# Value products, row-sum product and shift rows in tiles of 32 output columns, and one mask product placed earlier

## The chip, the core and the metric

The kernel runs on one core of one Trainium2 chip. A core has a matrix engine (TensorE; PE in the profile, with its weight loads shown apart as PEld), a vector engine (VectorE, DVE), an activation engine (ScalarE, ACT), a general engine (GpSimd, POOL) and an engine that issues transfers (SyncE, SP). SBUF is the working memory, PSUM the memory into which TensorE writes its products. The metric is the device time of one execution in microseconds; less is better.

## The reference: what is computed

Two blocks follow one another. The first is attention with routing, for 4 batches of 8 heads, 768 positions, head size 64:

```
q_assign = argmax(q_n @ c_n.T);  k_assign = argmax(k_n @ c_n.T)     # 16 centroids a head
mask     = q_assign[:, None] == k_assign[None, :]
scores   = where(mask, q @ k.T / 8, -1e9)
attn     = exp(scores - rowmax);  attn = attn / (sum(attn) + 1e-9)
out      = attn @ v
```

Its output, seen as x of 3072 tokens by 512, goes into the second block, `g = h * erf(softplus(h))` with `h = x @ w_in` (512 by 2048), and `out = g @ w_out` (2048 by 512). All matrices are float32.

## The kernel before, in words

Heads are taken in pairs (`e` = 0, 1 on partitions 0 to 63 and 64 to 127): 16 pairs `p`. Within a pair the queries are two halves of `HW` = 384 columns and the keys six tiles `j` of 128, so that a pair has 12 units (pair, half, j). A unit's scores stand with keys on partitions and queries along the free axis, `[128, 2, 384]`. The main loop is `period(p, i)`, i = 0 to 5, which carries two units u and u+1. Each engine executes in the order in which the code emits (the wrapper `InOrder`), and no planner moves anything. In a period, in the order of emission on TensorE:

- `turn` (in i = 0 and 3): six small products of `lowest`, the row maxima of three query tiles, bring the shifts of a half into a row; two ACT copies put it into `qm`.
- `step_ahead(u)`: for the next half to come, a tile of 128 queries by 384 keys in bf16 into the one PSUM tile `wide`, two products `qv,kv` and two mask products `qm,km`; DVE takes the row maximum (`nmx`).
- `products(u)`, `products(u+1)`: the float32 scores, two matmuls a unit, into one of two PSUM tiles `sc`.
- `step_ahead(u+1, True)` in two parts, `scores(u)` beside its second, then `scores(u+1)`: bf16 mask products onto the scores.
- `mask(place)`: `MASKS` says in which period and at which of four places (0 to 3) the mask operands `qm`, `km` of the next pair are made, by one product of `hotT` and `pick` into a `turned` tile and one copy (on DVE in i = 0, else on ACT). Before, the keys' first is at (0, 2), that is after `scores(u+1)`; its copy comes after that of the row maxima on DVE.
- `similarities(p+2)` (i = 3): four matmuls of 32 output columns by 384 moving columns, in tiles of 32 columns already.
- `curve(u)`, `curve(u+1)`: ACT's exponential of `sc` into one of eight SBUF tiles `pr`, each with two extra columns of a tiny constant behind the 384.
- `accumulate(u-2)`, `accumulate(u-1)`: POOL sums the `pr` tiles of a half over j into `acc`.
- `attend(u-2)`, `attend(u-1)` (the change's "second products"): v times `pr`, for each head one float32 matmul of 64 output columns by 386 moving columns, summed over j in the PSUM tile `turned[half]`.
- `divide` (i = 0 and 3, once a half): the "sums' product", `minus` (all -1, 64 columns) times `acc`, into `turned[1 - half]`. It gives the negative row sum, the same on all 64 partitions of a head. Then ACT makes the reciprocal by logarithm and exponential (`inv`), DVE makes `den`, scales the product in place (`raw`) and writes `x`, and SP sends `x` to the transposed activations `x_dram`. Its later parts are emitted in the next period.

Two `turned` tiles serve for attend's sums, the sums' product, the similarities, the masks and the shift rows. Beside all this ACT, DVE and POOL round the weights of the second block and make forms of them (until pair 11 or so, and from pair 12 on).

After pair 15 the second block runs on float32 products of 128 by 128 by 256, seven products for eight (`block`). Its first block of products comes before the last `divide` (`finish_attention`).

In the trace each float32 matmul shows as two passes, each with a weight load; a bf16 matmul is one pass. All work recorded by the wrapper has line 60.

Of the kernel before, what the change touches and what calls it, by code (L numbers as in the profile page):

```python
# [9 lines left out]
F32 = mybir.dt.float32  # L10
# [4 lines left out]
ALU = mybir.AluOpType  # L15
ACT = mybir.ActivationFunctionType
# [3 lines left out]
P = 128  # L20
B, H, S, D = 4, 8, 768, 64
C = 16
NJ = S // P
Q = 32
NB = S // Q
HW = S // 2
HJ = NJ // 2
HP = H // 2
NPAIR = B * HP
# [14 lines left out]
EPS = 2.0**-70  # L44
NPT = NJ + 2
N_LATE = 10
LAST_X = 11
MASKS = {(0, 2): ("k", 0), (2, 0): ("q", 0), (2, 2): ("k", 1), (5, 2): ("q", 1)}
FIRST_MASKS = {(2, 0): ("k", 0), (2, 1): ("q", 0), (2, 2): ("k", 1), (5, 2): ("q", 1)}


# [17 lines left out]
def kernel(  # L69
# [10 lines left out]
    nc = tc.nc  # L80

    in_order = [True]
    te, ve, ae, ge = (
        InOrder(tc, e, in_order) for e in (nc.tensor, nc.vector, nc.scalar, nc.gpsimd)
    )
# [4 lines left out]
    const = pool("const", 1)  # L90
# [3 lines left out]
    turned = [ps.tile([P, 512], F32, name=f"turned{i}") for i in range(2)]  # L94
# [3 lines left out]
    more_in = const.tile([P, 3, HK, DFF // 2], F32, name="more_in")  # L98
    more_out = const.tile([P, 3, HF, HM], F32, name="more_out")
    x_more = const.tile([P, 3, HK, HT], F32, name="x_more")  # L100
    minus = const.tile([P, D], F32, name="minus")
    alleps = const.tile([P, 1], F32, name="alleps")
    x_dram = dram.tile([DM, B * S], F32, name="x_dram")

# [8 lines left out]
    const = passing("fixed", 1)  # L113
    stage = passing("stage", 1)
    vp = passing("vp", 2)
    routep = passing("routep", 1)
# [18 lines left out]
    def part_of(i, lo, n):  # L135
        return more_out[:, i].rearrange("p f m -> p (f m)")[:, lo : lo + n]
# [1 line left out]
    rows = [{nm: const.tile([P, S], F32, name=f"{nm}T{i}") for nm in "qk"} for i in range(2)]  # L138
    rows.append({"q": part_of(1, 2 * HW, S), "k": part_of(2, 2 * HW, S)})

    prs = [const.tile([P, 2, HW + 2], F32, name=f"pr{i}") for i in range(NPT)]


    pairs = {}
# [31 lines left out]
        load(p, "k", k, stage if p != 1 else None)  # L176


    setup = prs[-1].rearrange("p e n -> p (e n)")
    cen = setup[:, 0:D]  # L180
    sy.dma_start(out=cen, in_=centroids.rearrange("h c d -> (h c) d"))

# [6 lines left out]
    make_identity(nc, ident)  # L189
    ve.memset(ccT, 0.0)  # L190
    for t in prs:
        ge.memset(t[:, :, HW : HW + 2], EPS)

    ge.memset(first, -1.0)
    for base, pattern, sign, op, fill in (
# [67 lines left out]
    for e in range(2):  # L263
        for n in range(2):
            r = e * D + n * Q
# [9 lines left out]
        ge.memset(t, 0.0)  # L275

    cn = setup[:, D : 3 * D].rearrange("p (e d) -> p e d", e=2)
    spare = iter(range(3 * D, HW))

    def scalar_tile():  # L280
        n = next(spare)
# [73 lines left out]
    def masks(p, nm, half, bank, narrow=False, copied_by=ae):  # L355

        if p >= NPAIR:
            return lambda: None
        st = pairs[p]
        cols = slice(half * HW, (half + 1) * HW)  # L360
        r = slice(0, D) if nm == "q" else slice(D, P)
        if narrow:
            r = slice(r.start + half * Q, r.start + (half + 1) * Q)
        won = bank[:, 0:HW]
        te.matmul(won, lhsT=pick[r, half], rhs=st["hotT"][r], start=True, stop=True)
        if nm == "q":
            return lambda: ae.activation(out=st["qm"][:, cols], in_=won, func=ACT.Relu)
        if copied_by is ve:
            return lambda: ve.tensor_scalar(
                out=st["km"][:, cols], in0=won, scalar1=BIG, scalar2=nbig, op0=ALU.mult, op1=ALU.add  # L370
            )
        return lambda: ae.activation(
            out=st["km"][:, cols], in_=won, func=ACT.Identity, bias=nbig, scale=BIG
        )
# [3 lines left out]
    def maxima_step(p, i, sm=wide, behind=False):  # L378

        st = pairs[p]  # L380
        nmx = maxima[p % 2]
        t, half = divmod(i, 2)

        def passes(a, b, start, rows):
            for e in range(2):
                r = slice(e * D + rows.start, e * D + rows.stop)
                te.matmul(
                    sm[:, e, 0:HW], lhsT=st[a][r, t * P : (t + 1) * P],
                    rhs=st[b][r, half * HW : (half + 1) * HW], start=start, stop=not start,
                )  # L390

        passes("qv", "kv", True, slice(0, D))
        if behind:
            yield
        passes("qm", "km", False, slice(Q, D) if behind else slice(0, D))
        ve.tensor_reduce(
            out=nmx[:, :, t, half], in_=sm[:, :, 0:HW], axis=AX.X, op=ALU.max, negate=True
        )
        if i in (NJ - 1, 2 * NJ - 1):
            h = i // NJ  # L400
            ve.tensor_reduce(
                out=lowest[h][:, :, ::D].rearrange("p t e -> p e t"),
                in_=nmx[:, :, h * HJ : (h + 1) * HJ], axis=AX.X, op=ALU.min,
            )
            turns.append((p, h))

    def turn(p, h, copies=(ae.copy, ae.copy)):

        st = pairs[p]
        pn = turned[h][:, 0:HW].rearrange("p (t n) -> p t n", t=HJ)  # L410
        for t in range(HJ):
            for e in range(2):
                cols = slice(e * D, (e + 1) * D)
                te.matmul(pn[cols, t], lhsT=lowest[h][:, t, cols], rhs=identb, start=True, stop=True)
        for e, copy in zip(range(2), copies):
            r = slice(e * D, e * D + 1)
            copy(out=st["qm"][r, h * HW : (h + 1) * HW], in_=pn[r].rearrange("p t n -> p (t n)"))
        st["shift", h] = True
# [6 lines left out]
    sc_of = {}  # L425
# [14 lines left out]
    def scores(u):  # L440

        p, half, j = units[u]
        st = pairs[p]
        sc = sc_of[u]
        assert ("shift", half) in st
        for e in range(2):
            r = slice(e * D, (e + 1) * D)
            r = slice(r.start, r.start + Q)
            te.matmul(
                sc[:, e, 0:HW], lhsT=st["km"][r, j * P : (j + 1) * P],  # L450
                rhs=st["qm"][r, half * HW : (half + 1) * HW], start=False, stop=True,
            )

    def curve(u):

        pr = prs[u % NPT]
        ae.activation(out=pr[:, :, 0:HW], in_=sc_of.pop(u)[:, :, 0:HW], func=ACT.Exp, scale=D**-0.5)

    def accumulate(u):

        p, half, j = units[u]
        st = pairs[p]
        pr = prs[u % NPT]
        if j == 1:
            st["acc", half] = part_of(1 + half, 0, 2 * HW).rearrange("p (e t) -> p e t", e=2)
        if j > 0:
            acc = st["acc", half]
            so_far = prs[(u - 1) % NPT][:, :, 0:HW] if j == 1 else acc
            ge.tensor_tensor(out=acc, in0=so_far, in1=pr[:, :, 0:HW], op=ALU.add)

    def attend(u):

        p, half, j = units[u]
        st = pairs[p]
        if j == 0:
            st["av", half] = turned[half][:, 0 : HW + 2]
        for e in range(2):
            te.matmul(
                st["av", half][e * D : (e + 1) * D], lhsT=st["v"][:, j, e], rhs=prs[u % NPT][:, e],
                start=(j == 0), stop=(j == NJ - 1),  # L480
            )

    def divide(u):

        p, half, _ = units[u]
        st = pairs[p]
        av = st["av", half]

        psum = turned[1 - half][:, 0:HW]
        for e in range(2):  # L490
            te.matmul(
                psum[e * D : (e + 1) * D], lhsT=minus, rhs=st["acc", half][:, e], start=True, stop=True
            )

        if u + 1 < len(units):
            inv = routep.tile([P, HW], F32, name="inv")
            den = routep.tile([P, HW], F32, name="den")
        else:
            inv, den = part_of(0, 4 * HW, HW), part_of(1, 0, HW)
        ae.activation(out=inv, in_=psum, func=ACT.Ln, bias=alleps, scale=-1.0)  # L500
        ae.activation(out=inv, in_=inv, func=ACT.Exp, scale=-1.0)
        yield
        ve.scalar_tensor_tensor(
            out=den, in0=psum, scalar=S * EPS, in1=inv, op0=ALU.subtract, op1=ALU.mult
        )
        raw = av[:, 0:HW]
        ve.scalar_tensor_tensor(
            out=raw, in0=raw, scalar=av[:, HW : HW + 1], in1=inv, op0=ALU.add, op1=ALU.mult
        )
        yield  # L510
        x = part_of(0, (2 * p + half) % 4 * HW, HW)
        ve.scalar_tensor_tensor(out=x, in0=den, scalar=2.0, in1=raw, op0=ALU.add, op1=ALU.mult)
        b, r = divmod(p, HP)
        nc.sync.dma_start(
            out=x_dram[r * P : (r + 1) * P, b * S + half * HW : b * S + (half + 1) * HW], in_=x
        )
        if half == 1:
            del pairs[p]
        yield
# [222 lines left out]
    def period(p, i):  # L742
# [4 lines left out]
        def mask(place):  # L747
            which = (MASKS if p else FIRST_MASKS).get((i, place))
            if which:
                return masks(p + 1, *which, turned[0 if i in (0, 5) else 1], place > 1, ve if i == 0 else ae)  # L750
            return lambda: None

        if u > 0:
# [13 lines left out]
        second = step_ahead(u + 1, True) if u > 0 else iter(())  # L767
        next(second, None)
        scores(u)
        next(second, None)  # L770
        next(part[0], None)
        scores(u + 1)
# [59 lines left out]
                next(part[0])  # L832
        if i == 3 and early(n2):
            size(n2)
        mask(3)()


    def warm(n, bank, rhs):
# [176 lines left out]
```

## Time and profile before

| what | value |
|---|---|
| median of 3 runs | 1011.37 us (1010.65 to 1011.74) |
| the profiled execution | 1011.8 us |
| its span, first to last instruction | 1009.3 us |
| PE busy over the span | 1001.3 us (99%) |
| DVE, ACT, POOL busy over the span | 699.8, 501.6, 349.2 us |
| from 30 to 424 us (attention): PE, DVE, ACT, POOL busy | 394.0, 310.0, 288.5, 304.7 us of 394.0 |
| from 424 us to the end: PE busy | 581.8 us of 585.3 |
| granted TensorE clock | 1.00 |
| x_dram writes (line 514) | 32 of 192 KB, 2.0 us from issue to landing |

A group's row reads: engine and operation, out<-in by the program's names, the tile of the array in rows*columns and shapes, how many, busy time in us and the mean length of one in ns. Lengths of passes overlap: TensorE is pipelined, so the time that a pass costs is read from one start to the next and not from its length.

### The profile page before, as it was taken

To read this page: it belongs to the slowest core of one execution; us is meant where nothing else is said; L and a number is where in the kernel's file an instruction comes from. 1 tells how busy PE (TensorE), PEld (TensorE's weight loads), DVE (VectorE), ACT (ScalarE), POOL (GpSimd) and SP (SyncE) were. 2 spreads that over 40 slices of the span, in tenths; PEclk is the share of its full clock that TensorE was granted. 3 is DMA by queue.
4 is the path that set the end of the run, shared out by engine and by line. 5 is a ranking of instruction groups with operands and counts; after the bars stand their busy time and mean duration, and the time that the engine had idled before them with its cause. 6 is when DMAs were issued, how large, how long until landed. Compare 5 with 4: busy or idle time off the path is not lost.

```text
span 1009.3 us, 15518 instructions
## 1 busy us (share of the span) xinstructions
PE 1001.3 (99%) x5930; PEld 699.8 (69%) x5930; DVE 699.8 (69%) x1315; ACT 501.6 (50%) x659; POOL 349.2 (35%) x237
## 2 busy tenths in 40 slices
PE   8999999999999999999999999999999999999998
PEld 3444444444444444488888888888888888888887
DVE  8788888888788776869767564756565647565653
ACT  3777777777777665467623222232314050505050
POOL 1677777777777777853120000000000000000000
PEclk9999999999999999999999999999999999999999
DMA  9444444444344211042001100110001000000001
GB/s 208 90 104 103 104 102 101 104 104 106 84 106 101 55 33 32 23 169 84 0 1 43 43 1 1 42 42 1 21 22 42 0 22 21 1 1 21 22 1 42
DMA packets 141641, 55.55 MB, mean 55 GB/s; under 512 B 127104, under 2 KB 131456, under 8 KB 141568
## 3 DMA queue, kind: packets, MB, share of 16 engines
q1 hardware_dynamic: 139216, 54.28, 21.0%
q8 instruction: 46, 0.75, 0.3%
q10 hardware_dynamic: 2352, 0.30, 0.2%
q14 instruction: 27, 0.22, 0.1%
HBM read 41.98 MB, written 12.58 MB: 54 GB/s over the span
## 4 chain that ended last, share of the span: by engine, by line
PE 96%; DVE 2%; DMA 1%; SPq 0%; issue 0%; ACT 0%; DVEq 0%; ACTq 0%
PE bank L60 43%; PE turned L60 32%; PE sc L60 16%; PE wide L60 5%; DVE nmx L60 1%; DMA in_k<-in_k_dram 0%; SPq L60 0%; DMA in_q<-in_q_dram 0%; DVE x_own L60 0%; DVE more_in L60 0%; DVE x_more L60 0%; DVE w_in L60 0%; DVE kT L60 0%; DVE turned L60 0%; DVE sims L60 0%
## 5 line engine op out<-in xcount | busy, mean ns | idle before, releaser
L60 DVE TENSOR_REDUCE nmx<-wide 128x2 f32<-128x768 f32 x189 | 180.9, 957 | 80.7 <-PE wide L60 80.0
L60 POOL TENSOR_TENSOR more_out<-more_out,pr 128x768 f32<-128x768 f32 x128 | 216.4, 1691 | 28.7 <-ACT pr L60 22.8
L60 ACT ACTIVATE pr<-sc 128x768 f32<-128x768 f32 x192 | 148.8, 811 | 91.0 <-PE wide L60 86.6
L60 PE MATMUL turned<-pr,in_v 128*64 128x386 f32 x768 | 145.4, 500 | 0.0
L60 DVE TENSOR_TENSOR g<-bank,g 128x256 f32<-128x256 f32 x222 | 89.7, 422 | 53.1 <-PE bank L60 46.5
L60 PE MATMUL bank<-x_own,w_in 128*128 128x256 f32 x424 | 104.6, 380 | 0.5 <-DVE x_own L60 0.5
L60 PE MATMUL bank<-w_out,g 128*128 128x256 f32 x448 | 103.1, 379 | 0.0
L60 PE MATMUL sc<-qT,kT 64*128 64x384 f32 x528 | 98.2, 484 | 0.0
L60 PEld LDWEIGHTS turned<-pr,in_v 128*64 128x64 f32 x768 | 46.6, 136 | 69.9 <-issue 59.3
L60 PEld LDWEIGHTS bank<-w_out,g 128*128 128x128 f32 x448 | 85.1, 190 | 11.6
L60 PEld LDWEIGHTS bank<-x_own,w_in 128*128 128x128 f32 x424 | 80.3, 190 | 12.9 <-DVE x_own L60 0.9
L60 ACT COPY g<-bank 128x256 f32<-128x256 f32 x28 | 10.4, 372 | 152.4 <-PE bank L60 148.4
L60 DVE TENSOR_TENSOR osb<-bank,osb 128x256 f32<-128x256 f32 x87 | 35.5, 421 | 72.8 <-ACT osb L60 25.4
L60 ACT ACT_TABLE_LOAD x48 | 61.6, 1283 | 45.7 <-DVE g L60 45.1
L60 PE MATMUL bank<-x_more,more_in 128*128 128x256 f32 x296 | 76.0, 379 | 0.0
L60 PEld LDWEIGHTS <-qv 64*128 64x128 bf16 x384 | 26.8, 93 | 68.5 <-issue 52.5
L60 POOL TENSOR_TENSOR more_out<-pr,pr 128x768 f32<-128x768 f32 x32 | 59.3, 1854 | 28.4 <-ACT pr L60 28.4
L60 PEld LDWEIGHTS sc<-qT,kT 64*128 64x128 f32 x528 | 52.4, 187 | 19.9 <-ACT pr L60 1.2
L60 PE MATMUL wide<-kv,qv 64*128 64x384 bf16 x378 | 64.8, 328 | 1.1 <-ACT km L60 0.6
L60 PE MATMUL bank<-more_out,g_more 128*128 128x256 f32 x272 | 64.3, 379 | 0.0
L60 DVE TENSOR_TENSOR g<-a_s,g 128x512 f32<-128x512 f32 x96 | 62.5, 689 | 1.4 <-ACT a_s L60 1.4
L60 PE MATMUL wide<-km,qm 64*128 64x384 bf16 (+1 forms) x378 | 62.5, 327 | 0.0
(170 smaller groups left out, 1683.5 us busy)
## 6 DMA issues: line engine op xcount, KB each, us to landing
x_own<-in_moe_w_in_dram SPq DMA_DIRECT2D x13, 512.0 KB, 4.5
in_v<-in_v_dram SPq DMA_DIRECT2D x32, 192.0 KB, 2.9
x_dram<-more_out SPq DMA_DIRECT2D x32, 192.0 KB, 2.0
x_own<-x_dram SPq DMA_DIRECT2D x6, 1024.0 KB, 5.1
out_dram<-osb SPq DMA_DIRECT2D x23, 256.0 KB, 2.0
in_k<-in_k_dram SPq DMA_DIRECT2D x59, 96.0 KB, 2.7
in_q<-in_q_dram SPq DMA_DIRECT2D x58, 96.0 KB, 2.7
g_more<-in_moe_w_out_dram SPq DMA_DIRECT2D x6, 512.0 KB, 3.5
```

What stands on the lines that cost most here:

```text
L60: ins = getattr(self.engine, name)(*args, **kw)
```

## The change

It does five things. `pr` is laid out as quarters, for each head two runs of 192 queries with the two extra columns behind each (`TW` = 194). `attend` splits each head's matmul into four: two parts `k` of 32 output columns by two runs `c` of 194 moving columns; the four (head, run) combinations `g` go to the four 32-column tiles of the array, and `k` is placed along the free axis of PSUM. The sums' product uses `minus` with 32 columns and the four quarters of `acc` as moving operands, so it writes 32 equal rows for each quarter. What follows it works on that layout: `den` and `inv` have 192 columns, `raw` is two instructions, and `x` leaves in four transfers. `turn` takes 32 columns of `lowest` instead of 64. And the keys' first mask product moves from place 2 to place 3 of period 0, which now lies between `scores(u)` and `scores(u+1)`; its DVE copy comes before the row maximum of `step_ahead(u+1)`.

```diff
+QW = HW // 2
+TW = QW + 2
...
-MASKS = {(0, 2): ("k", 0), (2, 0): ("q", 0), (2, 2): ("k", 1), (5, 2): ("q", 1)}
+MASKS = {(0, 3): ("k", 0), (2, 0): ("q", 0), (2, 2): ("k", 1), (5, 2): ("q", 1)}
...
-    minus = const.tile([P, D], F32, name="minus")
+    minus = const.tile([P, Q], F32, name="minus")
...
-    prs = [const.tile([P, 2, HW + 2], F32, name=f"pr{i}") for i in range(NPT)]
+    prs = [const.tile([P, 2, 2, TW], F32, name=f"pr{i}") for i in range(NPT)]
...
         passes("qm", "km", False, slice(Q, D) if behind else slice(0, D))
+        if behind:
+            yield
         ve.tensor_reduce(
...
-                cols = slice(e * D, (e + 1) * D)
+                cols = slice(e * D, e * D + Q)
                 te.matmul(pn[cols, t], lhsT=lowest[h][:, t, cols], rhs=identb, start=True, stop=True)
...
-        ae.activation(out=pr[:, :, 0:HW], in_=sc_of.pop(u)[:, :, 0:HW], func=ACT.Exp, scale=D**-0.5)
+        sc = sc_of.pop(u)[:, :, 0:HW].rearrange("p e (c x) -> p e c x", c=2)
+        ae.activation(out=pr[:, :, :, 0:QW], in_=sc, func=ACT.Exp, scale=D**-0.5)
+
+    def quarters(t):
+        return t.rearrange("p e c n -> p (e c) n")[:, :, 0:QW]
...
-            st["av", half] = turned[half][:, 0 : HW + 2]
-        for e in range(2):
-            te.matmul(
-                st["av", half][e * D : (e + 1) * D], lhsT=st["v"][:, j, e], rhs=prs[u % NPT][:, e],
-                start=(j == 0), stop=(j == NJ - 1),
-            )
+            st["av", half] = turned[half][:, 0 : 2 * TW].rearrange("p (k n) -> p k n", k=2)
+        for k in range(2):
+            for g in range(4):
+                te.matmul(
+                    st["av", half][g * Q : (g + 1) * Q, k], lhsT=st["v"][:, j, g // 2, k * Q : (k + 1) * Q],
+                    rhs=prs[u % NPT][:, g // 2, g % 2], start=(j == 0 and k == 0), stop=(j == NJ - 1 and k == 1),
+                )
...
-        psum = turned[1 - half][:, 0:HW]
-        for e in range(2):
-            te.matmul(
-                psum[e * D : (e + 1) * D], lhsT=minus, rhs=st["acc", half][:, e], start=True, stop=True
-            )
+        psum = turned[1 - half][:, 0:QW]
+        for g in range(4):
+            te.matmul(psum[g * Q : (g + 1) * Q], lhsT=minus, rhs=st["acc", half][:, g], start=True, stop=True)
...
-        raw = av[:, 0:HW]
+        for k in range(2):
+            raw = av[:, k, 0:QW]
+            ve.scalar_tensor_tensor(
+                out=raw, in0=raw, scalar=av[:, k, QW : QW + 1], in1=inv, op0=ALU.add, op1=ALU.mult
+            )
+        yield
+        x = part_of(0, (2 * p + half) % 4 * HW, HW).rearrange("p (k x) -> p k x", k=2)
         ve.scalar_tensor_tensor(
-            out=raw, in0=raw, scalar=av[:, HW : HW + 1], in1=inv, op0=ALU.add, op1=ALU.mult
+            out=x, in0=den.unsqueeze(1).to_broadcast([P, 2, QW]), scalar=2.0, in1=av[:, :, 0:QW],
+            op0=ALU.add, op1=ALU.mult,
         )
...
-        nc.sync.dma_start(
-            out=x_dram[r * P : (r + 1) * P, b * S + half * HW : b * S + (half + 1) * HW], in_=x
-        )
+        for g in range(4):
+            rows_of, at = r * P + g // 2 * D, b * S + half * HW + g % 2 * QW
+            nc.sync.dma_start(
+                out=x_dram[rows_of : rows_of + D, at : at + QW].rearrange("(k r) x -> r k x", k=2),
+                in_=x[g * Q : (g + 1) * Q],
+            )
...
-                return masks(p + 1, *which, turned[0 if i in (0, 5) else 1], place > 1, ve if i == 0 else ae)
+                return masks(p + 1, *which, turned[0 if i in (0, 5) else 1], place > 1, ve if place == 3 else ae)
...
         scores(u)
+        next(second, None)
+        mask(3)()
         next(second, None)
         next(part[0], None)
         scores(u + 1)
...
         if i == 3 and early(n2):
             size(n2)
-        mask(3)()
```

More of the change, by code (lines that the diff above doesn't have):

```diff
@@ L176, in load_qk @@
         load(p, "k", k, stage if p != 1 else None)
-    setup = prs[-1].rearrange("p e n -> p (e n)")
+    setup = prs[-1].rearrange("p e c n -> p (e c n)")
     cen = setup[:, 0:D]
@@ L191 @@
     for t in prs:
-        ge.memset(t[:, :, HW : HW + 2], EPS)
+        ge.memset(t[:, :, :, QW:], EPS)
     ge.memset(first, -1.0)
@@ L277 @@
     cn = setup[:, D : 3 * D].rearrange("p (e d) -> p e d", e=2)
-    spare = iter(range(3 * D, HW))
+    spare = iter(range(TW, HW))
     def scalar_tile():
@@ L464, in accumulate @@
         if j == 1:
-            st["acc", half] = part_of(1 + half, 0, 2 * HW).rearrange("p (e t) -> p e t", e=2)
+            st["acc", half] = part_of(1 + half, 0, 2 * HW).rearrange("p (g x) -> p g x", x=QW)
         if j > 0:
             acc = st["acc", half]
-            so_far = prs[(u - 1) % NPT][:, :, 0:HW] if j == 1 else acc
-            ge.tensor_tensor(out=acc, in0=so_far, in1=pr[:, :, 0:HW], op=ALU.add)
+            so_far = quarters(prs[(u - 1) % NPT]) if j == 1 else acc
+            ge.tensor_tensor(out=acc, in0=so_far, in1=quarters(pr), op=ALU.add)
     def attend(u):
@@ L487, in divide @@
         av = st["av", half]
-        psum = turned[1 - half][:, 0:HW]
-        for e in range(2):
-            te.matmul(
-                psum[e * D : (e + 1) * D], lhsT=minus, rhs=st["acc", half][:, e], start=True, stop=True
-            )
+        psum = turned[1 - half][:, 0:QW]
+        for g in range(4):
+            te.matmul(psum[g * Q : (g + 1) * Q], lhsT=minus, rhs=st["acc", half][:, g], start=True, stop=True)
         if u + 1 < len(units):
-            inv = routep.tile([P, HW], F32, name="inv")
-            den = routep.tile([P, HW], F32, name="den")
+            inv = routep.tile([P, QW], F32, name="inv")
+            den = routep.tile([P, QW], F32, name="den")
         else:
-            inv, den = part_of(0, 4 * HW, HW), part_of(1, 0, HW)
+            inv, den = part_of(0, 4 * HW, QW), part_of(1, 0, QW)
         ae.activation(out=inv, in_=psum, func=ACT.Ln, bias=alleps, scale=-1.0)
@@ L505, in divide @@
         )
-        raw = av[:, 0:HW]
+        for k in range(2):
[5 more added lines that the diff above has]
+        x = part_of(0, (2 * p + half) % 4 * HW, HW).rearrange("p (k x) -> p k x", k=2)
         ve.scalar_tensor_tensor(
-            out=raw, in0=raw, scalar=av[:, HW : HW + 1], in1=inv, op0=ALU.add, op1=ALU.mult
-        )
-        yield
-        x = part_of(0, (2 * p + half) % 4 * HW, HW)
-        ve.scalar_tensor_tensor(out=x, in0=den, scalar=2.0, in1=raw, op0=ALU.add, op1=ALU.mult)
+            out=x, in0=den.unsqueeze(1).to_broadcast([P, 2, QW]), scalar=2.0, in1=av[:, :, 0:QW],
+            op0=ALU.add, op1=ALU.mult,
+        )
         b, r = divmod(p, HP)
-        nc.sync.dma_start(
-            out=x_dram[r * P : (r + 1) * P, b * S + half * HW : b * S + (half + 1) * HW], in_=x
-        )
+        for g in range(4):
[4 more added lines that the diff above has]
+            )
         if half == 1:
```

## Prediction, made before the changed kernel was run

> **What bounds the kernel now.** I read the page's busy times first, then its chain and groups, then the timeline of TensorE around `divide`.
>
> ```profile
> PE 1001.3 (99%) x5930; PEld 699.8 (69%) x5930; DVE 699.8 (69%) x1315; ACT 501.6 (50%) x659; POOL 349.2 (35%) x237
> ...
> PE 96%; DVE 2%; DMA 1%; SPq 0%; issue 0%; ACT 0%; DVEq 0%; ACTq 0%
> ...
> L60 PE MATMUL turned<-pr,in_v 128*64 128x386 f32 x768 | 145.4, 500 | 0.0
> ```
>
> PE is busy all the time and the chain stays on it for 96%. Between 30 and 424 us it is busy 394.0 of 394.0 us; DVE 310.0, POOL 304.7, ACT 288.5. A pair takes 25.50 us, each like the last. So what counts is the distance from one PE start to the next. Period 3, then period 0, each with `divide`:
>
> ```profile
> 288.13 0.52 PE L60 MATMUL turned<-qT,ccT 128*32 128x384 f32 x2
> 288.14 0.52 PE L60 MATMUL turned<-kT,ccT 128*32 128x384 f32 x2
> 288.48 0.49 PE L60 MATMUL turned<-qT,ccT 128*32 128x384 f32 x2
> 288.49 0.49 PE L60 MATMUL turned<-kT,ccT 128*32 128x384 f32 x2
> 288.91 1.52 PE L60 MATMUL turned<-pr,in_v 128*64 128x386 f32 x8
> 290.26 0.82 PE L60 MATMUL turned<-more_out,minus 128*64 128x384 f32 x4
> 291.01 0.34 PE L60 MATMUL wide<-kv,qv 64*128 64x384 bf16 x2
> ```
>
> ```profile
> 301.90 0.61 DVE L60 TENSOR_SCALAR km<-turned,nbig 128x384 bf16<-128x384 f32 x1
> ...
> 302.63 0.23 PEld L60 LDWEIGHTS turned<-more_out,minus 128*64 128x64 f32 x4 [0.61 <-issue]
> 302.66 0.87 PE L60 MATMUL turned<-more_out,minus 128*64 128x384 f32 x4
> ...
> 303.46 0.34 PE L60 MATMUL wide<-kv,qv 64*128 64x384 bf16 x2
> ```
>
> What to see. (1) In the similarities, four tiles of 32 columns run at once: four passes start within 0.02 us and the next four 0.347 us later. (2) In narrow windows the attend passes start in pairs at 288.91, 289.29, 289.61, 289.94: steps of 0.375, 0.324, 0.324. A float32 pass thus streams two PE cycles a column (386 in 0.322) plus 2 ns; the first step of a group carries the exposed weight load, 0.053 for 64 columns and 0.027 (0.347 - 0.320) for 32. (3) From the last pass to the next work it is 0.32 if that uses the same tile shape (288.91 to 290.26 is 1.35), and 0.42 if it doesn't: a change of shape costs 0.10. (4) A sums' product takes 290.26 to 291.01 = 0.75: one step of 0.324, the last pass 0.324, and the change. (5) In period 0 it starts 0.138 later than in period 3 (0.456 after the last attend pass instead of 0.318): its PSUM tile is still read by the km copy on DVE, 301.90 to 302.51. That delay stands in 14 periods 0, those of pairs 1 to 14.
>
> **What the Trainium skill says.** "TensorE: Matmul & The Clock Gate", section "Packing small matmuls — row/col tiling": matmuls in different column tiles run side by side, starting about 4 ns apart; the similarities show 7 ns, four in 0.02 us. Its section "Wait — 56ns, not 53.3ns?" gives about 2.5 ns a matmul above streaming (here 2) and a floor near 25 ns between starts; no run here shows that floor. "TensorEngine Tiling (Array Packing)", section "Key Properties": changing the tiling mode drains the array; here that is the 0.10.
>
> **The change, part by part.** Times in us of PE's path.
>
> *Attend.* Two units: before, 8 passes in four pairs; after, 32 passes in eight rounds of four, 194 x 2 / 2.4 GHz = 0.162 + 0.002 = 0.164 a round. Before, first start to next work of another shape: 0.375 + 2 x 0.324 + 0.007 + 0.420 = 1.450. After: first step 0.189, six of 0.164, 0.020 between the first and the fourth tile, last pass and change 0.260: 1.453. So 0 within 0.02, in 96 groups. The streamed work is the same, and the loads hide: 32 columns occupy 0.027 of a 0.164 round. Unknown is whether PE can issue eight records (four loads, four passes) each 0.164 for over a microsecond; before, attend needs four per 0.324. Below, I bound it at +0.7 a group (see the rivals); above, no gain, since streaming sets the step. I take 0.
>
> *Sums' product.* Before 4 passes of 384 columns on two tiles, after 8 of 192 on four: half the streaming, as 64 equal rows become 32. Two steps of 0.324 become two of 0.162: -0.323. There are 32 (128 passes by 4); the last lies in the second block. 31 x 0.323 = 10.0, with the last 10.3.
>
> *Same shape after the similarities.* In period 3 the similarities now have attend's shape: 0.416 from their last start to attend becomes about 0.302 (same step as any, less the stagger), and attend's first load hides, 0.189 to 0.164. Together 0.14, in 14 pairs: -2.0.
>
> *Mask product moved.* Same row tile and shape between `scores(u)` and `scores(u+1)`: no PE cost; it may wait for hotT (DVE 300.12 to 300.69) about 0.01. Its copy now runs on DVE near 301.12 to 301.7 instead of 301.90 to 302.51; the sums' product, wanted near 302.51, finds its tile free, and POOL's last sum ends at 301.48. The 0.138 goes: 14 x 0.138 = -1.9. Queued behind the copy is the row maximum of `step_ahead(u+1)`, 0.53 later than now; `wide` is wanted again 1.47 after that maximum's end, less the 0.5 gained: covered. If it were not, 0.1 a pair. `scores(u+1)` goes back 0.16 behind the mask; `curve(u)` (0.8) covers that.
>
> *Shift rows.* Six passes in three steps of 0.056 either way, set by 128 moving columns: 0.
>
> *DVE, ACT, POOL, SP.* From 512 to 256 columns a DVE float32 operation falls 0.69 to 0.42, 1.03 ns a column, so `den` 0.55 to 0.35, `raw` 0.62 to two of 0.42; `x` stays at 0.545. In issue distance that is 1.00 to about 0.93. ACT's two fall by 0.14 each (0.75 ns a column, from 811 at 768 and 524 at 384). `curve` and POOL keep their 768 elements in rows of 192; should rows cost, each has over 20% idle. `x` leaves in four transfers instead of one, some 1.5 more of SP a half (0.34 to 0.49 an issue); loads queued behind have most of a pair before they are read. None of these is on the path.
>
> *What is late next.* The row maximum must end before the second use of `wide` in a period. It ends 0.125 before it almost everywhere, some 0.05 of which is the shortest distance seen: 0.07 spare. In period 4 the maximum now starts 0.25 after DVE went idle (291.30), and PE arrives 0.46 earlier. DVE can overlap it by 0.09, so it is 0.12 late, of which 0.07 is spare: 0.05 a pair given back where weights are rounded, 11 x 0.05 = 0.6.
>
> Sum: -10.3 - 2.0 - 1.9 + 0.6 = -13.6, attend 0 +- 2. Span 1009.3 - 13.6 = 995.7; the profiled execution 1011.8 - 13.6 = 998.2; the median lies 0.4 below the profiled one, so 997.8.
>
> **Rivals.**
>
> *DVE takes half back.* For it: DVE has 310 of 394 us, 19.9 in a pair of 25.5, and after the change of 24.6; one PSUM tile `wide` couples it to PE with 0.07 to spare, and the copy now stands before a row maximum. In periods 0, 1, 3 and 4 a delay of 0.1 each gives 0.4 a pair, 6.4 in all, and a similar wait in front of `turn`, where `lowest` comes just in time, up to 2: 1003 to 1005. Against it: the slacks in periods 1 and 2 come out positive when I follow DVE through.
>
> *Attend slows, and the kernel with it.* If issue, not streaming, sets the round of four, seven steps a group stretch in 96 groups. The gain is used up at 13.6 / (96 x 7) = 0.020 a step: a round of 0.184, 46 ns for a load and a pass. At the skill's 62 ns a matmul without hardware decode (the section named) a round would be 0.248, +0.59 a group (with the last step 0.67): +56 to +64, so about 1055. For it: the trace never shows such a rate for long; its densest microsecond holds 29 records, half of what attend would need (49). Against it: twelve records within 0.05 us in the similarities, and 24 in half a microsecond, so the queue can run ahead, and over a whole period the rate needed is only 104 records in 4.3 us.
>
> *It doesn't do what it says.* If column tiles reading four different halves of `pr` shared a stream, attend would double; the similarities already read four different runs at full rate, so this is in the last rival's chance. No difference at all would need attend to lose just the gain.
>
> **How the numbers follow.** Full gain, 994 to 1000.5: 0.65, its own range. Half taken back by DVE, or attend a few per cent slower, 1000.5 to 1008: 0.21. Slower than before by attend: 0.10. More gain than I see, below 994: 0.02. Same: 0.02. The likeliest gives 997.8. The range 993.5 to 1005 holds the first case and most of the second. Faster by over 0.2% (2 us, about what a measurement of this kernel can tell) 0.88, same 0.02, slower 0.10.
>
> **What would show it.** Right: attend passes in 128*32 with rounds 0.164 apart; the group for `minus` in 128*32, with 0.43 from its first pass to `wide`; `minus` 0.16 after the last attend round in period 0 too; a pair of about 24.6 us; PE still busy without gaps. Wrong: attend rounds over 0.184 apart; PE idle or late behind nmx in periods 1 and 4, seen as row maxima without idle before them and second uses of `wide` 0.05 after them; ACT waiting long for `sc`.

## The result, and the profile after

The changed kernel takes 997.23 us (median of 4 runs, 997.00 to 997.93) where the kernel before takes 1011.56 (its three runs and a fourth of 1011.88): a ratio of 0.986, 95% interval 0.984 to 0.988. The forecast was 997.8. The profiled execution took 997.0 us, its span is 995.3, 14.0 less than before. The medians of the kernel before in the experiments lie lower, between 1011.13 and 1011.19, so medians that differ by half a microsecond or less say little; there the distances in the traces decide.

The page of the changed kernel, its busy times and attend's group; then the sums' product from the list of groups with shapes kept apart:

```profile
PE 987.6 (99%) x8362; PEld 743.0 (75%) x8362; DVE 700.5 (70%) x1347; ACT 488.0 (49%) x659; POOL 350.3 (35%) x237
...
L62 PE MATMUL turned<-pr,in_v 128*32 128x194 f32 x3072 | 145.5, 330 | 0.0
```

```profile
L62 PE MATMUL turned<-more_out,minus 128*32 128x192 f32 x256 | 16.3, 326 | 0.0
```

PE is still busy throughout. Attend has four times as many passes and the same busy time as before, 145.5 against 145.4 us; the sums' product has twice as many passes and 16.3 against 26.8 us. The mean length of a pass says little: it is 330 ns, and rounds of four passes follow each other 0.164 us apart.

The timeline of PE in period 3 of a pair (start us, length us, operation, how many), from the similarities to the next period:

```profile
82.18 0.52 PE L62 MATMUL turned<-qT,ccT 128*32 128x384 f32 x2
82.19 0.52 PE L62 MATMUL turned<-kT,ccT 128*32 128x384 f32 x2
82.53 0.49 PE L62 MATMUL turned<-qT,ccT 128*32 128x384 f32 x2
82.54 0.49 PE L62 MATMUL turned<-kT,ccT 128*32 128x384 f32 x2
82.85 1.50 PE L62 MATMUL turned<-pr,in_v 128*32 128x194 f32 x32
84.16 0.51 PE L62 MATMUL turned<-more_out,minus 128*32 128x192 f32 x8
84.60 0.34 PE L62 MATMUL wide<-kv,qv 64*128 64x384 bf16 x2
```

From the first pass of `minus` to `wide` it is 0.441 us instead of 0.748. From the similarities' last pass to attend it is 0.303 instead of 0.416, now that both have the same tile shape. The same view of all engines in period 0, lines between left out:

```profile
70.23 1.52 PE L62 MATMUL turned<-pr,in_v 128*32 128x194 f32 x32
70.25 0.62 DVE L62 TENSOR_SCALAR km<-turned,nbig 128x384 bf16<-128x384 f32 x1 [0.51 <-PE turned L62]
70.79 0.95 DVE L62 TENSOR_REDUCE nmx<-wide 128x2 f32<-128x768 f32 x1
...
71.57 0.51 PE L62 MATMUL turned<-more_out,minus 128*32 128x192 f32 x8
...
72.01 0.34 PE L62 MATMUL wide<-kv,qv 64*128 64x384 bf16 x2
```

The km copy ends at 70.87, well before `minus` wants the tile at 71.57, and `minus` follows the last attend round without a wait.

Where the 14.0 us went, read from the distances between attend's first passes in pairs 1 to 11 (medians):

| stretch | before, us | after, us | difference |
|---|---|---|---|
| period 0's attend to period 1's | 4.595 | 4.089 | -0.506 |
| period 2's attend to period 3's (holds the similarities) | 4.720 | 4.595 | -0.125 |
| period 3's attend to period 4's | 4.405 | 4.117 | -0.288 |
| the three others together | 11.78 | 11.79 | +0.01 |
| a whole pair | 25.50 | 24.587 | -0.913 |

The similarities are in 14 of 16 pairs, and 14 times 0.913 is 12.8. The last two pairs, which have none, bring 1.0 together; what is left, about 0.2, lies in single pairs and in the start. The last sums' product, in the second block, brings nothing: from the first pass of the last attend group to the end it is 587.95 us before and 587.94 after. PE is done with it 0.33 sooner and then waits for `g` on DVE:

```profile
416.35 0.53 PE L62 MATMUL turned<-more_out,minus 128*32 128x192 f32 x8
416.81 1.13 PE L62 MATMUL bank<-x_own,w_in 128*128 128x256 f32 x4
...
418.74 1.13 PE L62 MATMUL bank<-x_own,w_in 128*128 128x256 f32 x4 [0.80 <-DVE g L62]
```

### The profile page after: what moved, and what is told of

Read it like the earlier page. It is cut to its first block, busy times and chain, and to the rows that moved or that the text cites. A ratio compares the mean times of both kernels' runs of the same rounds, so it can differ in the third digit from the quotient of the medians.

```text
span 995.3 us, 20543 instructions
## 1 busy us (share of the span) xinstructions
PE 987.6 (99%) x8362; PEld 743.0 (75%) x8362; DVE 700.5 (70%) x1347; ACT 488.0 (49%) x659; POOL 350.3 (35%) x237
## 4 chain that ended last, share of the span: by engine, by line
PE 96%; DVE 1%; POOL 1%; DMA 1%; issue 0%; ACT 0%; SPq 0%; ACTq 0%; DVEq 0%; POOLq 0%
PE bank L62 43%; PE turned L62 31%; PE sc L62 16%; PE wide L62 6%; POOL more_out L62 1%; DVE nmx L62 1%; DMA g_more<-in_moe_w_out_dram 0%; DMA in_q<-in_q_dram 0%; DVE sims L62 0%; POOL x_more L62 0%; DVE kT L62 0%; DVE qT L62 0%; ACT pr L62 0%; ACT w_out L62 0%; DVE turned L62 0%
## 5 line engine op out<-in xcount | busy, mean ns | idle before, releaser
L62 PE MATMUL turned<-pr,in_v 128*32 128x194 f32 x3072 | 145.5, 330 | 0.0
L62 PEld LDWEIGHTS turned<-pr,in_v 128*32 128x32 f32 x3072 | 91.5, 109 | 51.2 <-issue 21.3
```

The costliest lines, as they stand in the source:

```text
L62: ins = getattr(self.engine, name)(*args, **kw)
```

## The experiments

**Every sums' product twice.** If this product lies bare on PE's path, doubling it must cost what halving it brought.

```diff
-        for g in range(4):
+        for g in [0, 1, 2, 3] * 2:
             te.matmul(psum[g * Q : (g + 1) * Q], lhsT=minus, rhs=st["acc", half][:, g], start=True, stop=True)
```

> The changed kernel with every sums' product computed twice over (the same four matmuls again), all else alike. My theory: the sums' product lies bare on TensorE's path and two passes of 192 columns cost 0.162 each, so +0.325 us in each of 32 places: +10.4, less some 0.5 because the row maximum of period 4 is then no longer late: 1007.1 us, and 0.32 us more from the first pass of minus to wide. If the gain of the change came from elsewhere and the sums' product is covered by waits: within 2 us of 997.2.

Measured: 1006.56 us, +9.3 on the changed kernel. PE's timeline in period 3:

```profile
85.40 0.83 PE L62 MATMUL turned<-more_out,minus 128*32 128x192 f32 x16
86.17 0.34 PE L62 MATMUL wide<-kv,qv 64*128 64x384 bf16 x2
```

First pass to `wide` is 0.766, 0.325 more, as expected; the sum expected, +9.9, was a little too large. A pair is 25.183, 0.596 longer: two times 0.325 less 0.054, because PE, now later in period 4, no longer has to wait there (its second use of `wide` comes 0.124 after the row maximum's end, not 0.053). The last product, doubled too, lengthens the way from the last attend group to the end by 0.10 only. So each two rounds of 192 columns are worth 0.325 in 31 places, and the halving of the streamed columns is the largest part of the gain.

**Attend and shift rows in 64 columns again, sums' product left narrow.**

```diff
-                cols = slice(e * D, e * D + Q)
+                cols = slice(e * D, (e + 1) * D)
...
-        for k in range(2):
-            for g in range(4):
-                te.matmul(
-                    st["av", half][g * Q : (g + 1) * Q, k], lhsT=st["v"][:, j, g // 2, k * Q : (k + 1) * Q],
-                    rhs=prs[u % NPT][:, g // 2, g % 2], ...
+        for e in range(2):
+            te.matmul(
+                turned[half][e * D : (e + 1) * D, 0 : 2 * TW], lhsT=st["v"][:, j, e],
+                rhs=prs[u % NPT][:, e].rearrange("p c n -> p (c n)"), ...
```

> The changed kernel with attend (64 output columns by 388 moving columns, two matmuls a unit) and the shift rows (64 columns) as they were; the sums' product stays in four tiles of 32 columns by 192. Queries and output columns then stand on other partitions than the reciprocals that they are divided by, so the division is by the wrong sums; the work is the same in amount. My theory: attend itself costs the same either way, and what is lost is the shared tile shape: +0.10 us between attend and the sums' product in 32 places (+3.2) and +0.14 after the similarities in 14 places (+2.0), less some 0.5 to 0.9 for slack: about 1001.5 us. Rival: attend's finer tiles bring the gain themselves; then it returns to about 1007 or more.

Measured: 1003.13 us, +5.9 instead of +4.3.

```profile
83.85 1.52 PE L62 MATMUL turned<-pr,in_v 128*64 128x388 f32 x8
85.31 0.53 PE L62 MATMUL turned<-more_out,minus 128*32 128x192 f32 x8
85.77 0.34 PE L62 MATMUL wide<-kv,qv 64*128 64x384 bf16 x2
```

Attend to `wide` in a period without `divide` is 1.457, against 1.453 in four tiles: attend itself costs the same. What is lost is 0.141 in period 0 (attend to the sums' product), and 0.129 and 0.113 in the two stretches at period 3. The rival, that the finer attend brings the gain, is out; but a change of shape costs more than the 0.10 that I had put down, because behind it the first weight load also shows (0.465 from `minus` to `wide`, 0.024 more than 0.441).

**Only the shift rows in 64 columns again.**

```diff
-                cols = slice(e * D, e * D + Q)
+                cols = slice(e * D, (e + 1) * D)
```

> The changed kernel with only the shift rows in tiles of 64 columns again. My theory: narrowing them saves nothing by itself, but keeps them in attend's tile shape; undone, each costs a change of shape, 0.10 us in some 31 places: +3.1, 1000.3 us, with about 0.24 instead of 0.144 from the last attend pass to the first of lowest. Rival: a change between 32 and 64 columns costs nothing and only that between row and column tiles does: 997.2 us.

Measured: 1001.12 us, +3.9.

```profile
78.32 1.52 PE L62 MATMUL turned<-pr,in_v 128*32 128x194 f32 x32
79.78 0.36 PE L62 MATMUL turned<-identb,lowest 128*64 128x128 bf16 x6
80.06 0.34 PE L62 MATMUL wide<-kv,qv 64*128 64x384 bf16 x2
```

From the last attend round to the first pass of `lowest` it is 0.258 instead of 0.144, and the stretch is 0.126 longer; 31 x 0.126 = 3.9. So a change between 64 and 32 columns costs time as well, and six small products in the wrong shape cost a quarter of the whole change's gain.

**The mask product back in its old place in the changed kernel, and moved alone in the kernel before.**

```diff
-MASKS = {(0, 3): ("k", 0), ...
+MASKS = {(0, 2): ("k", 0), ...
```

> The changed kernel with the keys' first mask product back behind the second unit's scores, all else alike. My theory: the sums' product of period 0 waits again for the copy on VectorE in 14 pairs, about 0.14 us each: +1.9, 999.1 us, seen as about 0.28 instead of 0.144 from the last attend pass to minus. Rival: with the finer tiles the place makes no difference, within 0.5 us of 997.2.

> The kernel before with only the keys' first mask product moved between the two units' scores. My theory: -0.138 us in 14 pairs, 1009.6 us. Rival: VectorE's row maximum, now behind the copy, gives it back as a wait at the next use of wide: 1011.5 us or more.

Measured: back in its place, 999.52 us, +2.3 on the changed kernel; moved alone in the kernel before (with the `yield` and the place-3 call of the change), 1008.56 us against 1011.17 in the runs beside it, a ratio of 0.997 (0.996 to 0.998), -2.6. The first, period 0, all engines:

```profile
71.14 0.61 DVE L62 TENSOR_SCALAR km<-turned,nbig 128x384 bf16<-128x384 f32 x1
...
71.90 0.53 PE L62 MATMUL turned<-more_out,minus 128*32 128x192 f32 x8
...
72.36 0.34 PE L62 MATMUL wide<-kv,qv 64*128 64x384 bf16 x2
```

`minus` starts 0.291 after the last attend round instead of 0.144, behind the copy that ends at 71.75, and the stretch to the next attend is 0.172 longer. In the kernel before, the move takes 0.189 from it: `minus` 0.318 after the last attend pass instead of 0.456, and 0.747 instead of 0.798 from there to `wide`. There PE's load of `minus` starts only after the wait, 0.03 before its first pass and not 0.2 as in period 3, and the second round comes late; the wait's 0.138 was not its whole price. Neither rival held: the place matters, and no wait behind the row maximum takes its gain back.

**Attend in passes of 97 columns.** This measures how fast PE can be fed.

```diff
         for k in range(2):
-            for g in range(4):
+            for lo, hi in ((0, TW // 2), (TW // 2, TW)):
+                for g in range(4):
...
```

(the moving operand, the output and `start`/`stop` follow `lo` and `hi`)

> The changed kernel with each attend matmul of 194 moving columns split into two of 97, so 64 passes a group of two units instead of 32, with the same streamed columns. It measures what issue can do: eight records in 0.083 us if streaming still sets the pace. If streaming does: about +0.02 us a group, 999 us. If a record costs more than 0.0104 us in a long run: each 0.001 us more adds 0.128 us a group, 12 us in all; at the 25 ns between starts of matmuls that the Trainium skill names (TensorE: Matmul & The Clock Gate, section Wait - 56ns, not 53.3ns?), if it holds over all tiles together, 64 x 0.025 = 1.6 us a group instead of 1.33, about 1023 us.

Measured: 999.63 us, +2.4.

```profile
83.21 1.52 PE L62 MATMUL turned<-pr,in_v 128*32 128x97 f32 x64
84.55 0.51 PE L62 MATMUL turned<-more_out,minus 128*32 128x192 f32 x8
```

Sixteen rounds about 0.083 apart; a group without `divide` takes 1.304 + 0.177 = 1.481, 0.028 more than 1.453, and 96 x 0.028 = 2.7. Four loads and four passes each 0.083 us, 10 ns a record, went through for 1.3 us on end. The slow side of my forecast, issue as the bound of attend, would have needed 23 ns a record; it is excluded for groups of this length. The floor near 25 ns between starts that the prediction took from the Trainium skill ("TensorE: Matmul & The Clock Gate", section "Wait — 56ns, not 53.3ns?") does not hold over different column tiles: here passes start 21 ns apart on average. The similarities, with starts 7 ns apart, had shown that before. Within one tile passes start about 0.084 us apart here, so that no run tests the floor there.

**Two weight operations moved into DVE's idle time in period 2.** The one loss that I had forecast is in period 4: PE's second use of `wide` at 86.27 comes 0.053 after the row maximum ends, the least distance there is. DVE's timeline of the changed kernel:

```profile
83.90 0.38 DVE L62 TENSOR_SCALAR w_in<-w_in 128x512 uint32<-128x512 uint32 x1
84.21 0.55 DVE L62 TENSOR_REDUCE sc<-sims 128x24 f32<-128x384 f32 x1
84.79 0.55 DVE L62 TENSOR_TENSOR hot<-sims,sc 128x384 bf16<-128x384 f32 x1
85.26 0.95 DVE L62 TENSOR_REDUCE nmx<-wide 128x2 f32<-128x768 f32 x1
```

Before the change DVE stood idle 0.25 before that row maximum; now it doesn't. So I moved `bounded` and `shifted` out of period 3.

```diff
             step_ahead(u)
+        if i == 2 and early(n1):
+            bounded(n1)
+            shifted(n1)
...
         elif i == 3 and early(n1):
-            bounded(n1)
             sign(n1)
...
-            if early(n1):
-                shifted(n1)
```

> The changed kernel with two weight operations of VectorE moved from period 3 to the start of period 2, where it idles. My theory: the row maximum of period 4 is 0.05 us late in 11 pairs in the changed kernel; without these two in front of it it isn't: -0.5 us, 996.7 us, and a pair of 24.54 instead of 24.59. If the lateness has another cause: 997.2 us and pairs of 24.59.

Measured: 1012.40 us, +15.2 on the changed kernel and a little slower than the kernel before (ratio 1.001, 1.0005 to 1.0018). DVE, POOL and PE in period 2:

```profile
51.41 7.08 POOL L62 TENSOR_TENSOR more_out<-more_out,pr 128x768 f32<-128x768 f32 x4
...
52.52 2.69 DVE L62 TENSOR_SCALAR w_in<-w_in 128x512 f32<-128x512 f32 x2
...
55.12 0.94 DVE L62 TENSOR_REDUCE nmx<-wide 128x2 f32<-128x768 f32 x1
56.10 0.19 DVE L62 TENSOR_REDUCE lowest<-nmx 128x6 bf16<-128x18 f32 x1
...
56.34 0.34 PE L62 MATMUL turned<-identb,lowest 128*32 128x128 bf16 x6 [1.25 <-DVE lowest L62]
```

The two operations, 0.42 and 0.38 in period 3, take 2.69 together beside POOL's sums; the row maximum and the shifts come late, and PE stands still for about 1.25 us in each of 11 pairs. A pair is 25.965, 1.378 longer; 11 x 1.378 = 15.2. The part of the theory that was about period 4 held in this run: the stretch from period 3 to 4 is 4.064, 0.053 shorter, and the distance there is 0.126 again. What failed is that DVE's idle time in period 2 could be used.

**The same, with POOL still.** Is it POOL?

```diff
-            for w in (u - 2, u - 1):
+            for w in (u - 2, u - 1) if i != 2 else ():
                 accumulate(w)
```

> The kernel with the two weight operations in period 2 (e7), and POOL's two sums of that period left out, so the row sums lack two of six key tiles. Theory A: the two operations took 2.7 us in place of 0.8 because POOL was at work on SBUF beside them; without its sums they take 0.4 each, and PE no longer waits for the shift rows: about 996.7 us. Theory B: they are long for another reason, such as what stands around them on VectorE; then they stay at 1 us or more each, and 1012 us.

Measured: 996.94 us. DVE in period 2 of the next pair:

```profile
77.49 0.88 DVE L62 TENSOR_SCALAR w_in<-w_in 128x512 f32<-128x512 f32 x2
78.54 0.96 DVE L62 TENSOR_REDUCE nmx<-wide 128x2 f32<-128x768 f32 x1 [0.17 <-PE wide L62]
```

0.88 us for both (2.70 in this pair with POOL at work), and the wait of PE is gone in all pairs but the first of them, where 0.33 is left. So it is POOL (theory A). The Trainium skill, page "SBUF — State Buffer", section "Who interferes with whom", says that GpSimd and a `tensor_scalar` of VectorE in a two-port mode exclude each other from a shared port pair for a whole instruction; the traces agree, with 2.69 us against 0.88, and beside POOL's sums each of the two, in all 11 pairs, ended 0.28 to 0.29 us after the end of one of POOL's additions. That they ran in the two-port mode no run here shows. With POOL still, period 4 can be judged too: the stretch from period 3 to 4 is 4.064 to 4.067 in all these pairs and a pair 24.535, 0.052 less than in the changed kernel, as the theory had it.

**x in one transfer.**

```diff
-        for g in range(4):
-            rows_of, at = r * P + g // 2 * D, b * S + half * HW + g % 2 * QW
-            nc.sync.dma_start(...)
+        nc.sync.dma_start(
+            out=x_dram[r * P : (r + 1) * P, b * S + half * HW : b * S + (half + 1) * HW],
+            in_=x.rearrange("p k x -> p (k x)"),
+        )
```

> The changed kernel with x written in one transfer a half instead of four; the quarters then go to wrong places in the transposed activations, the bytes are the same. My theory: the three further transfers are covered, 997.2 us within 0.3. Rival: SyncE's queue holds loads up: faster by more than 0.5 us.

Measured: 997.18 us, a span of 995.3 as in the changed kernel. The three further transfers a half are covered.

**One extra column instead of two.**

```diff
-TW = QW + 2
+TW = QW + 1
```

> The changed kernel with one extra column behind each quarter of pr instead of two, so attend has 193 moving columns instead of 194. If streaming alone sets attend's rounds: 2 cycles less in each of eight rounds, 0.0008 us, in 96 groups: -0.6 us, 996.6 us, with 1.187 instead of 1.193 from the first to the last pass of a group. If an uneven count costs something, above 997.2 us.

Measured: 996.77 us (996.74 to 996.87), the lowest median of all. A group is 1.188 from first to last pass instead of 1.193, a pair 24.560 instead of 24.587; 16 x 0.027 = 0.4. The ratio to the kernel before, 0.985 (0.984 to 0.987), overlaps that of the changed kernel, so only the traces tell the two apart.

## Why the prediction was right, and where it was off

*Attend, 0 within 0.02.* Right: 1.193 + 0.260 = 1.453 against 1.030 + 0.420 = 1.450 before, and 1.457 in 64 columns of output and 388 moving ones. Passes of 388, 194 and 97 columns came 0.326, 0.164 and about 0.084 apart, that is 0.83 ns a column and 2 ns a pass in both tile shapes. The exposed load of 32 columns is 0.024, not 0.027: that difference left out the 2 ns.

*Sums' product, -0.323 in 32 places.* Right in size in 31 of them: 0.325 for two rounds when doubled. The stretch from `minus` to `wide` fell by 0.307, because four tiles start 0.02 apart. Wrong in the last, in the second block: the 0.3 was counted without asking what PE does next, and there PE waits for DVE.

*Same shape after the similarities, -0.14.* Right: 0.416 to 0.303, and 1.193 to 1.169 within attend.

*Mask moved, -0.138 in 14 pairs.* Right in cause, too small: 0.189, by the mask moved alone. The step took the late start as the whole price; the timeline before had the rest in plain sight, 0.798 from `minus` to `wide` in period 0 against 0.748 in period 3. The missed 0.05 x 14 = 0.7 us would bring the forecast span from 995.7 to 995.0, and the 0.3 of the last sums' product, forecast and not found, back to the measured 995.3. So each mechanism was right but for that one place, and that the sum is off by 0.4 only is in part luck: two misses of opposite sign.

*Shift rows, 0.* Right as a difference, but the reason given was half of it. Narrowing them doesn't shorten them; it keeps them in attend's shape, which would else have cost 3.9.

*What is late next, +0.05 in 11 pairs.* Right: 0.054 by the doubled sums' product, 0.053 by the moved weight operations, with POOL at work and with POOL still.

*Durations on DVE.* `den` 0.351 (0.35 forecast), `raw` 0.426 each (0.42), `x` 0.544 (0.545).

*The rivals.* DVE took back 0.6 us of the path, not half of the gain. The issue of records, which held my chance of a slower kernel, isn't near a bound: attend needs a record about each 20 ns, and one each 10 ns went through. That streams of column tiles might be shared is out with attend's equal cost.

## What to carry to other kernels

On a kernel like this one, whose matrix engine hardly rests, count the streamed columns of each product, not its length or number: the product that wrote equal rows gave columns back in narrower tiles, and splitting the one that writes different rows gave nothing. Keep neighbours in one tile shape; small products between large ones count by the change of shape that they force. Before a gain is counted, ask whether PE would only wait longer behind it, as after the last sums' product. And DVE's idle time was free for these weight operations only where POOL rested; the row maxima, 0.93 to 0.96 us each beside the same additions of POOL, were not slowed.

## What the runs showed of the hardware that I had not expected

A change between 64 and 32 columns cost as much as one between row and column tiles: 0.114 us, 0.126 with the load behind it, against 0.10 before and 0.116 after the change. PE took a load or a pass every 10 ns over four column tiles for 1.3 us. And two `tensor_scalar` operations of 0.88 us together became 2.69 beside POOL's additions, enough to turn an expected gain of half a microsecond into a loss of 15. What may be the same, though no run tests it there, stood in the trace of the kernel before, for DVE's `tensor_tensor` at the end of attention, while POOL added and after it:

```profile
418.91 7.94 POOL L60 TENSOR_TENSOR more_out<-more_out,pr 128x768 f32<-128x768 f32 x4 [0.31 <-ACT pr L60]
...
425.23 2.16 DVE L60 TENSOR_TENSOR x_own<-x_own 128x512 f32<-128x512 f32 x1
427.32 0.68 DVE L60 TENSOR_TENSOR x_more<-x_more,x_own 128x512 f32<-128x512 f32 x1
```
